# Loading the early pair's table rows, and using them, three token tiles later

## The chip, the cores and the metric

The kernel runs on one core of one Trainium2 chip. The metric is the device time of one execution in microseconds; it is given as the median of three runs. Beside these there is one execution that the hardware profiler recorded, and all views of the profile are of that one.

## The reference

The program is an attention over pooled keys and values, followed by a layer of experts in which each token that passes a test goes to one expert out of eight.

```python
def _attn_ref(q, k, v):                       # 8 batches, 8 heads, 576 tokens, 64
    k_p = k.reshape(B, H, Sp, pool, D).mean(axis=3)          # pool = 8, Sp = 72
    v_p = v.reshape(B, H, Sp, pool, D).mean(axis=3)
    scores = scale * np.matmul(q, k_p.transpose(0, 1, 3, 2))
    attn = softmax(scores)
    return np.matmul(attn, v_p)

def _moe_ref(x, w_skip, w_gate, w1, w2):      # x: 4608 tokens of 512; 8 experts, F = 1024
    do_compute = x @ w_skip > 0
    out = x.copy()
    xc = x[do_compute]
    logits = xc @ w_gate
    e_idx = np.argmax(logits, axis=1)
    gate_w = softmax(logits)[arange, e_idx]
    for e in range(E):
        mask = e_idx == e
        h = np.maximum(xc[mask] @ w1[e], 0.0)
        y[mask] = gate_w[mask, None] * (h @ w2[e])
    out[do_compute] = xc + y
    return out
```

## The kernel before

The 4608 tokens are 36 tiles of 128. `attention` goes over them in a loop, `for t in range(NT)`, as a software pipeline written out by hand: in step t PE makes the scores of tile t (L295), ACT the exponentials of tile t - 1 (L309), PE the transposes of tile t - 2 (L320, L325), PE the products with v of tile t - 4 (`values`, L339 and L341, into the one PSUM tile `o`), and DVE normalises tile t - 5 (`normalised`: L353, L355, L359, L360). L360 writes the finished tile into `x`, a pool tile with three buffers, and L361 stores it on SP's queue into the result `out`.

PE, ACT and DVE run in the order of this code. POOL and SP take their work in the order in which it was given to them, each from a queue of its own. SP carries q (L283), k (L189), v (L217, L218), the weights of the first expert (L521), those of the second (L530), and the stores of x (L361). POOL pools v (L229 to L231), adds halves of k (L205), makes the low parts of the weights (`w2lo`, L540), places part of v (`vbd`, L272), and issues the indirect DMAs.

Beside this runs the routing, in groups of tiles (`GROUPS`, 6 tiles at first). `route` takes a group's logits through a chain of small DVE steps, a few in each t, and then scatters the token numbers and gate weights of each tile into a table in DRAM that is sorted by expert (`table`, L415, one indirect DMA for a tile on POOL's queue).

After 18 tiles (`EARLY`), the third group, `near_tokens` prepares a head start: the first 256 rows of the table belong to the first expert in `ORDER`, so a pair of 128-token tiles can be taken up before the routing is finished. L428 loads these rows into `near["ids"]` (`nids` in the trace) on SP's queue, L443 makes row numbers (`near["slot"]`, `nslot`) on DVE, and L445 gathers the two tiles of tokens from `out` into `ring[:, 3]` and `ring[:, 4]` by two indirect DMAs on POOL's queue. The DVE part and the gathers are put into `later` and run `NWAIT` = 3 steps of t after the last of the small steps of `near_tokens`.

What uses `ring` comes later: in the last two steps of the loop (t = 34, 35) `tx` transposes the two tiles on PE (L472) and copies them into `xhi` and `xlo`, and after the loop `products` runs the first layer (L482 to L484) and the second (L497 to L499) of that pair, between the last tiles' small steps. Then the table is complete, `slots` plans the rest, and `experts` works through all the experts' tokens.

Of the kernel before, what the change touches and what calls it, by code (L numbers as in the profile page):

```python
# [70 lines left out]
QUARTERS = 288, 320, 352, 384  # L71
HALF = 64
BIT = 3
NWAIT = 3
WARM = 3
SLOTS = 3 * (MAXU + 2)
NO_TOKEN = 1 << 20
# [81 lines left out]
def attention(tc, nc, q, k, vm, vr, cf, w1, w2, whi, wlo, out, c, pay, offs, table, load_constants, near, bufs, late, early, fin):  # L159
    with ExitStack() as ctx:  # L160
# [207 lines left out]
        def route(t0, n):  # L368
# [51 lines left out]
            if t0 + n == EARLY:  # L420
                yield from near_tokens()

        def near_tokens():

            count = offs[:, 0:1]
            less = ap.tile([128, 1], F32, name="less")
            nn = ap.tile([128, 1], F32, name="nn")
            nc.sync.dma_start(near["ids"], table[0:256].rearrange("(s l) t -> l s t", l=128))  # L428
            nc.vector.tensor_scalar(nn, count, 256.0, 2.0, ALU.is_ge, ALU.mult)
            yield  # L430
            nc.vector.tensor_scalar(less, count, 256.0, float(NO_TOKEN), ALU.is_lt, ALU.mult)
            yield
            nc.vector.tensor_scalar(near["first"][:, 0:1], nn, 128.0, None, ALU.mult)
            yield
            nc.vector.tensor_scalar(near["jt"][:, 0:1], nn, -1.0, float(JT), ALU.mult, ALU.add)
            yield
            nc.vector.tensor_tensor(near["place"], c["place"], nn, ALU.add)

            late("ring")
            nc.gpsimd.memset(bufs["ring"], 0.0)  # L440

            def gathers():
                nc.vector.tensor_scalar(near["slot"], near["ids"][:, :, 0], less, None, ALU.add)  # L443
                for i in range(2):
                    nc.gpsimd.indirect_dma_start(bufs["ring"][:, 3 + i, 0:D], None, out[0:EARLY * 128],  # L445
                                                 bass.IndirectOffsetOnAxis(ap=near["slot"][:, i:i + 1], axis=0),
                                                 bounds_check=EARLY * 128 - 1, oob_is_err=False)
            later[t + NWAIT] = gathers
            yield

        later = {}
# [232 lines left out]
        t = NT - 1  # L684
# [538 lines left out]
```

## Time and profile before

| what | value |
|---|---|
| median of three runs | 585.3 us (581.41, 585.3, 587.0) |
| the profiled execution | 581.93 us, its span 580.1 us |
| PE busy | 519.9 us (90% of the span) |
| PE weight loads busy | 466.2 us (80%) |
| DVE busy | 313.2 us (54%) |
| ACT busy | 245.2 us (42%) |
| POOL busy | 235.2 us (41%) |
| mean granted clock of PE | 0.957 |
| moved by DMA | 86.06 MB, mean 148 GB/s |

The span is the time from the first to the last instruction of the profiled execution; what is left to its time lies around it. A row of a timeline reads: start in us, duration in us, engine, line of the kernel, operation, what is written from what, the shape, how many such instructions were merged; in brackets the idle time ahead of it and what ended that. SPq is the sequencer that issues SP's DMAs. A row of a view of windows has, for each engine, its busy time in the window and the count of its instructions.

### The profile page before, as it was taken

The page shows a single profiled execution, that of the slowest core. Times are in us where ns is not written, and L with a number is a line of the kernel's source. Part 1 is how long each engine was busy: PE and PEld are TensorE (multiplying, and loading weights), DVE is VectorE, ACT ScalarE, POOL GpSimd, SP SyncE. Part 2 cuts the span into 40 slices and gives each one's busy share as a digit, 9 for nine tenths or more (in the row PEclk, how much of TensorE's full clock was granted, in tenths as well). Part 3 has the DMA queues.
Part 4 walks back from the last instruction along what each step waited for, and adds up shares of the span by engine and source line. Part 5 has one row for each costly group of instructions (what it writes and reads, how often), then busy time and mean ns, then how long its engine had stood idle before and what let it go on. Part 6 is the DMA issues. An engine that isn't in the chain of part 4 may idle for free. (4 is left out here: it accounts for less than half of the span.)

```text
span 580.1 us, 11104 instructions
## 1 busy us (share of the span) xinstructions
PE 519.9 (90%) x3347; PEld 466.2 (80%) x3348; DVE 313.2 (54%) x750; ACT 245.2 (42%) x672; POOL 235.2 (41%) x315
## 2 busy tenths in 40 slices
PE   8499978877499977699999999999999999999993
PEld 5398867767489956688898989989989898989892
DVE  3768778878367652124453545322363648465562
ACT  5478766758396101114141424212243436343440
POOL 4869386768852733111232123323242024204132
PEclk9799989879799998899999999999999999999998
DMA  8958996952768111001541235101144537562200
GB/s 300 398 219 294 317 193 251 238 206 78 254 198 239 57 38 44 7 20 57 201 156 56 74 145 185 60 31 52 54 142 170 187 117 255 184 236 97 91 26 7
DMA packets 33450, 86.06 MB, mean 148 GB/s; under 512 B 7486, under 2 KB 7747, under 8 KB 31489
## 3 DMA queue, kind: packets, MB, share of 16 engines
q1 hardware_dynamic: 25312, 71.62, 37.2%
q0 software_dynamic: 8096, 13.95, 7.1%
q8 instruction: 20, 0.33, 0.3%
q14 instruction: 22, 0.17, 0.1%
HBM read 73.79 MB, written 20.52 MB: 163 GB/s over the span
## 5 line engine op out<-in xcount | busy, mean ns | idle before, releaser
L1019 PE MATMUL psl<-xhi,w1hi 128*128 128x256 f32 (+3 forms) x416 | 122.7, 295 | 5.0 <-PEq L874 4.9
L1020 PE MATMUL psl<-xlo,w1hi 128*128 128x256 f32 (+3 forms) x416 | 122.1, 294 | 0.0
L1021 PE MATMUL psl<-xhi,w1lo 128*128 128x256 f32 (+3 forms) x416 | 122.0, 293 | 0.0
L949 POOL DMA_INDIRECT out<-ring,slot x39 | 39.4, 1011 | 188.3 <-POOLq L874 185.5
L1076 ACT ACTIVATE hhi<-psl 128x256 fp32r<-128x256 f32 (+4 forms) x104 | 42.0, 404 | 157.0 <-ACTq L874 155.9
L1033 PE MATMUL psf<-w2hi,hhi 128*128 128x512 f32 x240 | 96.7, 403 | 6.2 <-PEq L874 6.2
L1034 PE MATMUL psf<-w2lo,hhi 128*128 128x512 f32 x240 | 95.3, 397 | 0.0
L1133 DVE SCALAR_TENSOR_TENSOR hlo<-psl,hhi 128x256 fp32r<-128x256 f32 (+2 forms) x104 | 43.7, 422 | 80.6 <-DVEq L874 80.4
L1019 PEld LDWEIGHTS psl<-xhi,w1hi 128*128 128x128 f32 x416 | 78.8, 190 | 6.5 <-issue 5.9
L1036 PE MATMUL psf<-w2hi,hlo 128*128 128x512 f32 x200 | 79.6, 398 | 0.0
L1020 PEld LDWEIGHTS psl<-xlo,w1hi 128*128 128x128 f32 x416 | 78.9, 190 | 0.6
L1021 PEld LDWEIGHTS psl<-xhi,w1lo 128*128 128x128 f32 x416 | 78.9, 190 | 0.0
L339 PE MATMUL o<-vbd,pT 128*128 128x148 f32 (+1 forms) x304 | 54.1, 318 | 20.8 <-DVE x L360 17.5
L309 ACT ACTIVATE e<-sc,nm 128x72 f32<-128x72 f32 x288 | 64.8, 343 | 16.3 <-DVE nm L302 16.0
L1122 DVE SCALAR_TENSOR_TENSOR ring<-psf,ring 128x512 f32 x25 | 18.7, 749 | 83.9 <-DVEq L874 83.9
L339 PEld LDWEIGHTS o<-vbd,pT 128*128 128x128 f32 (+1 forms) x304 | 44.7, 197 | 23.5 <-issue 16.7
L1033 PEld LDWEIGHTS psf<-w2hi,hhi 128*128 128x128 f32 x240 | 45.5, 190 | 16.5 <-issue 6.6
L1034 PEld LDWEIGHTS psf<-w2lo,hhi 128*128 128x128 f32 x240 | 45.5, 190 | 9.9
L1085 ACT ACTIVATE xhi<-psd 128x512 fp32r<-128x512 f32 x36 | 18.9, 598 | 75.5 <-ACTq L874 75.5
L944 POOL DMA_INDIRECT ring<-out,slot x39 | 44.4, 1139 | 15.2 <-issue 12.9
L415 POOL DMA_INDIRECT table<-pay,r_di x36 | 35.7, 991 | 33.7 <-DVE rc L355 11.5
L1036 PEld LDWEIGHTS psf<-w2hi,hlo 128*128 128x128 f32 x200 | 37.9, 189 | 9.2
(207 smaller groups left out, 909.9 us busy)
## 6 DMA issues: line engine op xcount, KB each, us to landing
stage<-in_w SPq DMA_DIRECT2D x64, 512.0 KB, 4.4
out<-x SPq DMA_DIRECT2D x36, 256.0 KB, 4.9
stage<-in_k SPq DMA_DIRECT2D x7, 1152.0 KB, 9.8
hlo<-in_vm SPq DMA_DIRECT2D x4, 1024.0 KB, 8.4
hhi<-in_vm SPq DMA_DIRECT2D x4, 1024.0 KB, 5.4
xlo<-in_q SPq DMA_DIRECT2D x6, 512.0 KB, 6.7
qt<-in_q SPq DMA_DIRECT2D x6, 512.0 KB, 6.0
xhi<-in_q SPq DMA_DIRECT2D x5, 512.0 KB, 6.9
```

The costliest lines, as they stand in the source:

```text
L309: nc.scalar.activation(e[:, h, :], sc[h // 4][:, h % 4 * SP:(h % 4 + 1) * SP], AF.Exp, bias=nm[:, h:h + 1], scale=-1.0)
L339: nc.tensor.matmul(o_[sl, g * 2 * VA:(g + 1) * 2 * VA], pT[:, 2 * a + g, sl], vbd[b % 3][:, 2 * a + g, :], start=(g == 0), stop=False)
L944: g.indirect_dma_start(ring[:, s % 6, 0:D], None, out, bass.IndirectOffsetOnAxis(ap=slot[:, s:s + 1], axis=0), bounds_check=NTOK - 1, oob_ ...
L949: g.indirect_dma_start(out, bass.IndirectOffsetOnAxis(ap=offsets, axis=0), ring[:, s % 6, 0:D], None, bounds_check=NTOK - 1, oob_is_err=Fa ...
L1019: t.matmul(ps, whi[0][:, k, w], xhi[:, k, xs], start=(k == 0), stop=False)
L1020: t.matmul(ps, whi[0][:, k, w], xlo[:, k, xs], start=False, stop=False)
L1021: last = t.matmul(ps, wlo[0][:, k, w], xhi[:, k, xs], start=False, stop=(k == 3))
L1033: t.matmul(ps, hhi[:, k, sl], whi[1][:, k, :], start=(k == 0), stop=False)
L1034: last = t.matmul(ps, hhi[:, k, sl], wlo[1][:, k, :], start=False, stop=(short and k == 7))
L1036: last = t.matmul(ps, hlo[:, k, sl], whi[1][:, k, :], start=False, stop=(k == 7))
L1076: a.activation(hhi[:, f, xs], psL[f % 3][:, xs], AF.Relu).then_inc(sem["act"], 1)
L1133: m = v.scalar_tensor_tensor(to[:, f], psL[f % 3][:, cs], 0.0, hhi[:, f, cs].bitcast(F32), ALU.max, ALU.subtract)
```

## The change

The load of the table rows is taken out of the first of `near_tokens`' small steps and put into `later`, two steps of t (`NIDS`) after the last of them; the slot numbers and the gathers go from three steps after it to six.

```diff
-NWAIT = 3
+NIDS = 2
+NWAIT = 6
...
             nn = ap.tile([128, 1], F32, name="nn")
-            nc.sync.dma_start(near["ids"], table[0:256].rearrange("(s l) t -> l s t", l=128))
             nc.vector.tensor_scalar(nn, count, 256.0, 2.0, ALU.is_ge, ALU.mult)
...
             nc.gpsimd.memset(bufs["ring"], 0.0)
+
+            def ids():
+                nc.sync.dma_start(near["ids"], table[0:256].rearrange("(s l) t -> l s t", l=128))
 
             def gathers():
                 nc.vector.tensor_scalar(near["slot"], near["ids"][:, :, 0], less, None, ALU.add)
...
+            later[t + NIDS] = ids
             later[t + NWAIT] = gathers
             yield
```

The order of PE and of ACT stays as it was. On SP's queue, from the v load of the last batch (`hhi`, `vl`) on, the order before is this; `nids` is the load that moves, `stage<-in_w` are weights, `xhi`, `xlo` and `qt` with `in_q` are loads of q, and `out<-x` are stores of finished tiles:

```order
L217 DMA hhi<-in_vm 128x2048
L218 DMA vl<-in_vr 64x512
L428 DMA nids<-table 128x2x2
L521 DMA stage<-in_w 128x2x512
L283 DMA xhi<-in_q 128x1024
L361 DMA out<-x 128x512 x2
L521 DMA stage<-in_w 128x2x512
L283 DMA xlo<-in_q 128x1024
L361 DMA out<-x 128x512 x2
L283 DMA qt<-in_q 128x1024
```

And with the change (lines after the edit are four higher, one higher ahead of it):

```order
L218 DMA hhi<-in_vm 128x2048
L219 DMA vl<-in_vr 64x512
L525 DMA stage<-in_w 128x2x512
L284 DMA xhi<-in_q 128x1024
L362 DMA out<-x 128x512 x2
L525 DMA stage<-in_w 128x2x512
L284 DMA xlo<-in_q 128x1024
L362 DMA out<-x 128x512
L443 DMA nids<-table 128x2x2
L362 DMA out<-x 128x512
L284 DMA qt<-in_q 128x1024
```

The load of the table rows has gone behind two weight loads, two loads of q and three stores of x (tiles 21, 22 and 23).

On POOL's queue, at the end of the loop's work, the order before is this; `ring<-out,nslot` are the two gathers, `table<-pay,r_di` the scatters of the fourth routing group:

```order
L540 TENSOR_TENSOR w2lo<-stage,w2hi 128x512
L445 DMA ring<-out,nslot 128x512 x2
L272 TENSOR_TENSOR vbd_121<-gs,cfs 128x8x9
L275 TENSOR_TENSOR vl_124<-gs,cfs 64x4x9
L540 TENSOR_TENSOR w2lo<-stage,w2hi 128x512
L415 DMA table<-pay,r_di 36864x2 x6
L540 TENSOR_TENSOR w2lo<-stage,w2hi 128x512 x2
L272 TENSOR_TENSOR vbd_122<-gs,cfs 128x8x9
```

And with the change:

```order
L544 TENSOR_TENSOR w2lo<-stage,w2hi 128x512
L273 TENSOR_TENSOR vbd_121<-gs,cfs 128x8x9
L276 TENSOR_TENSOR vl_124<-gs,cfs 64x4x9
L544 TENSOR_TENSOR w2lo<-stage,w2hi 128x512
L416 DMA table<-pay,r_di 36864x2 x6
L544 TENSOR_TENSOR w2lo<-stage,w2hi 128x512 x2
L448 DMA ring<-out,nslot 128x512 x2
L273 TENSOR_TENSOR vbd_122<-gs,cfs 128x8x9
```

The gathers have gone behind the six scatters and three pieces of w2lo, and stand right ahead of the last batch's vbd. On DVE the one instruction that makes `nslot` has gone three steps of t later with them.

## The prediction

> **What bounds the kernel now.** I read the page's slices first, then SyncE's own waits, then the timelines of SP, DVE and PE around the one place that stands out, then POOL's timeline and the landings of its DMAs at the place to which work moves.
>
> ```profile
> span 580.1 us, 11104 instructions
> PE   8499978877499977699999999999999999999993
> SPq L428 <- DMA table<-pay,r_di: 15.1, 1, 15.1
> 129.49 0.47 SPq L218 DMA_DIRECT2D vl<-in_vr  x1
> 145.15 0.39 SPq L428 DMA_DIRECT2D nids<-table  x1
> 147.69 0.86 SPq L361 DMA_DIRECT2D out<-x  x2
> ```
>
> One slice is 14.5 us. From the eighteenth on PE is at nine tenths or more: the expert part is bound by PE and isn't touched by the change. The attention part before it has low slices, of which the eleventh, 145 to 160 us, is at four tenths. SP's queue explains that one: it meets the load of the table rows (nids, L428) at 130.0 us, and stands there for 15.1 us until the scatters into the table have landed. Behind it stand a weight load (L521), a load of q, and the stores of the finished token tiles (L361), which come out at 147.69.
>
> ```profile
> 141.80 0.68 DVE L360 TENSOR_TENSOR x<-o,rc 128x512 f32<-128x512 f32 x1
> 146.79 0.22 DVE L359 TENSOR_TENSOR l<-o,rc 128x72 f32<-128x72 f32 x1
> 153.28 0.69 DVE L360 TENSOR_TENSOR x<-o,rc 128x512 f32<-128x512 f32 x1 [6.27 <-DMA out<-x]
> 142.65 0.72 PE L339 MATMUL o<-vbd,pT 128*128 128x148 f32 x4
> 144.21 0.65 PE L295 MATMUL sc<-kbd,qt 128*128 128x144 f32 x4
> 144.70 0.60 PE L320 MATMUL pt<-cfs,e 128*128 128x128 f32 x4
> 145.84 0.76 PE L295 MATMUL sc<-kbd,qt 128*128 128x144 f32 x4
> 154.12 1.33 PE L339 MATMUL o<-vbd,pT 128*128 128x148 f32 x4 [7.53 <-DVE x L360]
> 157.22 1.03 PE L295 MATMUL sc<-kbd,xhi 128*128 128x144 f32 x4
> 158.08 0.30 PE L397 MATMUL mps<-r_oh,ones 128*128 128x56 bf16 x6
> ```
>
> This is the price. The tile x has three buffers; DVE's L360 may write tile 24 only when the store of tile 21 has landed, and that store left at 147.69 instead of soon after its x was ready. DVE waits 6.27 us, PE 7.53.
>
> **What the change takes away.** In the new order SP passes straight from the vl load to the weight load, the q load and the stores of tiles 21 and 22, then a weight load, a q load and the store of tile 23 before it meets nids. Tile 21's store can leave some 18 us before tile 24 needs the buffer (x of tile 24 is due at about 147). So L360 starts right behind L359, 0.15 us after its start as in the other tiles: 146.79 + 0.15 = 146.94 instead of 153.28, that is 6.34 us. There is a second part: after the gap PE runs slowly.
>
> ```profile
> 152.00:156.00 4.00, 1.88 (x8) 1.91 (x9) 2.49 (x9) 1.63 (x8) 2.62 (x3) 0.50 1.04 410
> 156.00:160.00 4.00, 4.00 (x31) 3.79 (x30) 1.64 (x7) 1.24 (x5) 2.10 (x2) 0.75 0.62 237
> ```
>
> The seventh figure after the window is the granted clock (0.50, then 0.75); the last two are DMA share and GB/s. The block of L339 and L341 takes 157.22 - 154.12 = 3.10 us there against 144.21 - 142.65 = 1.56 at full clock, and the scores behind it 158.08 - 157.22 = 0.86 against 144.70 - 144.21 = 0.49. That is 1.54 + 0.37 = 1.9 us that go too. **Term 1: -6.3 - 1.9 = -8.2 us.** What else is moved earlier here (two weight loads, two q loads) goes into a DMA that is quiet, and POOL's pooling of v that ran beside the stall now runs beside DVE, which I take to cost nothing that shows.
>
> ```profile
> 141.22 0.98 POOL L415 DMA_INDIRECT table<-pay,r_di  x1 [0.30 <-issue]
> 142.20 2.54 POOL L540 TENSOR_TENSOR w2lo<-stage,w2hi 128x512 fp32r<-128x512 f32 x2
> ```
>
> Nids itself now meets SP at about 145: the weight load ahead of it waits for a buffer that the first of these two w2lo sets free, at 143.5. The last scatter that nids needs is issued at 141.22 and had landed by 145.1, so with that landing SP hardly stops. Behind it stand the stores of tiles 24 and 25, a q load, and the first loads of the next expert's weights, none due for several us. I take 0; a rival below prices it.
>
> **What the change puts in its place.** The two gathers into ring (L445) leave POOL's place after w2lo and come behind six scatters of the next routing group and two more w2lo; DVE's one small L443 goes along and I take nothing for it. What uses the gathers doesn't move: the transposes of ring (L472) in the last two token tiles. On the old times, POOL and PE stand so there:
>
> ```profile
> 156.09 1.09 POOL L445 DMA_INDIRECT ring<-out,nslot  x1 [1.46 <-DVE nslot L443]
> 166.31 1.04 POOL L415 DMA_INDIRECT table<-pay,r_di  x1 [3.02 <-DVE pay L413]
> 172.80 0.98 POOL L415 DMA_INDIRECT table<-pay,r_di  x1 [0.30 <-issue]
> 173.79 2.52 POOL L540 TENSOR_TENSOR w2lo<-stage,w2hi 128x512 fp32r<-128x512 f32 x2
> 176.25 0.32 POOL L272 TENSOR_TENSOR vbd<-gs,cfs 128x72 f32<-128x72 f32 x1
> 175.83 0.60 PE L472 MATMUL mps<-cfs,ring 128*128 128x128 f32 x4
> 180.72 0.77 PE L339 MATMUL o<-vbd,pT 128*64 128x148 f32 x6 [0.44 <-DVE x L360]
> ```
>
> Both sides move 8.2 us earlier alike (POOL's scatters start at DVE's pay), so I compare them on the old times. The first gather is issued at about 176.3, when w2lo ends: PE wants its rows at 175.83. It is late before it has begun. When it lands is the question of this prediction. Alone, the two gathers took as the first line here says; a scatter takes as the second:
>
> ```profile
> DMA to landing us min/median/max: 2.1/2.6/3.1
> DMA to landing us min/median/max: 2.1/6.6/13.5
> table<-pay,r_di POOLq DMA_INDIRECT x1, 9.2
> table<-pay,r_di POOLq DMA_INDIRECT x1, 5.5
> table<-pay,r_di POOLq DMA_INDIRECT x1, 4.4
> table<-pay,r_di POOLq DMA_INDIRECT x1, 3.3
> 196.02 0.98 POOL L415 DMA_INDIRECT table<-pay,r_di  x1 [0.30 <-DVE r_cm L387]
> 198.59 0.98 POOL L415 DMA_INDIRECT table<-pay,r_di  x1 [0.30 <-issue]
> ```
>
> The third line is the scatter issued at 172.80, the sixth of the group that the gathers now follow: it lands at 182.0, with the weight loads of the next expert in flight. The next three are the scatters issued at 196.02, 197.31 and 198.59: they land at 201.5, 201.7 and 201.9, one closely behind the other. So DMAs of POOL's queue land in their order, and one behind a backlog comes out 0.2 us or so after the one ahead. I choose this over the lone gather's 2.6 us, because the new place is behind just such a group: the gather lands at 182.0 + 0.3 = 182.3. **Term 2: PE waits 182.3 - 175.8 = +6.5 us** at L472, with ACT, in order, behind it at the copy of those transposes. Bounds: +2.6 (a landing 2.1 us after issue) and +10.8 (the 13.5 us of the second line, 172.8 + 13.5 + 0.3 = 186.6). The second gather is wanted 3.8 us after the first and lands by then. On POOL the vbd of the last batch (L272) now stands behind two gathers, 1.09 + 0.3 + 1.0 = 2.4 us: 178.7 instead of 176.25, ahead of the L339 at 180.72 that needs it.
>
> **Term 3: the clock after that wait.** The gap of 7.53 us cost 1.9 us of slow PE. Shorter gaps went both ways:
>
> ```profile
> 110.65 1.32 PE L339 MATMUL o<-vbd,pT 128*128 128x148 f32 x4 [2.40 <-DVE x L360]
> 135.82 0.75 PE L339 MATMUL o<-vbd,pT 128*64 128x148 f32 x6 [2.93 <-DVE x L360]
> 136.00:140.00 4.00, 4.00 (x42) 3.79 (x41) 2.59 (x11) 2.76 (x11) 3.01 (x4) 1.00 0.06 3
> ```
>
> After 2.40 us the four L339 took 1.32 us, as slow as after the long gap; after 2.93 us the clock stayed at 1.00. Bounds 0 and 1.9; 6.5 us is nearest to 7.53, so **+1.9 us**.
>
> The Trainium skill, "TensorE: Matmul & The Clock Gate", Part 1, says that the PE clock falls to half after an idle window of about 3.4 us. This trace shows a fall after 2.40 us, so the row is stricter than the rule. By the rule a wait of 3.2 us, as in the first rival, would cost no clock.
>
> **Sum:** -8.2 + 6.5 + 1.9 = +0.2 us. The profiled execution took 581.93 us (span 580.1), so the sum is 582.1 on its own time. The three runs shown (581.41, 585.3, 587.0) and the profiled one have a mean of 583.9; with the sum that is **584.1 us**. No change, in other words: one long stall of PE traded for another.
>
> **Rivals.**
> The gather isn't held by the scatters. It lands 2.6 us after its issue, at 178.9, PE waits 3.1, and the clock costs half of its bounds, 1.0: -8.2 + 3.1 + 1.0 = -4.1, 579.8 us. For it: the lone gathers at 156 landed so right behind a stretch in which the DMA share was 1.04. Against it: the order of landings above.
>
> The Trainium skill, "DMA: Bandwidth & Descriptors", "Anatomy of one DMA — SWDGE (gpsimd) path", gives such a DMA about 2.0 us fixed and the bytes at 436 GB/s. An estimate from it for 256 KB is 2.6 us, which speaks for this rival; the scatters of this trace, with few bytes, took a median of 6.6.
>
> The same, and the drain gains. While PE waits, the last weight loads clear, and the scatters of the next groups find an empty DMA.
>
> ```profile
> 201.38 0.16 DVE L411 TENSOR_TENSOR r_di<-r_ds,r_no 128x2 int32<-128x2 f32 x1 [2.79 <-DMA table<-pay,r_di]
> ```
>
> This wait of 2.79 us for a landing then goes: -4.1 - 2.8 = -6.9, 577.0 us. Against it: six stores of x are in flight there before and after.
>
> Slower: a longer backlog. If the sixth scatter lands as the slowest of the first group did, PE waits 10.8: -8.2 + 10.8 + 1.9 = +4.5, 588.4 us. It decides from a wait of 6.3 us on, so from a landing at 182.1 on the old times, and the forecast sits just there. For it: one weight load now comes after the following store, so into the scatters' time. Against: 9.2 is what this group did.
>
> Slower: the stall stays at nids. The scatters that nids waits for landed 3.9 us after the last issue (141.22 to 145.1) in a DMA that SP's own stop kept empty; now loads run beside them. If the last one takes 13.5 us, SP is held until 154.7, the store of tile 24 lands 5.6 us later (as 147.69 to 153.28), at 160.3, and x of tile 27 (167.25 before, so 159.1) waits 1.2 us. With a clock loss of 1.9 the sum is 0.2 + 1.2 + 1.9 = +3.3, 587.2 us.
>
> ```profile
> 167.25 0.68 DVE L360 TENSOR_TENSOR x<-o,rc 128x512 f32<-128x512 f32 x1
> ```
>
> **How the numbers follow.** Forecast 0.38; gather not held 0.20; with the drain's gain 0.10; longer backlog 0.26; nids still blocking 0.06. One per cent, about what a measurement of this kernel can tell from no change, is 5.8 us. The case with the drain's gain is past it; of the first rival and the two slower ones, 4 to 5 us from nothing, I count a third to a half beyond it, since the runs of one kernel lie 5.6 us apart. That gives faster 0.2, same 0.6, slower 0.2. The range runs from the case with the drain's gain to the longer backlog, widened by the 3 us by which the runs lie about their mean: 576.5 to 591.5.
>
> **What would show it.** Right: SP's 15.1 us at nids shrinks to a few us, and tile 24's L360 has no wait for a store; PE's 7.53 us at L339 are gone; the transposes of ring wait 5 to 8 us for the gather, which lands 5 us or more after its issue; the granted clock is at half just behind. Wrong: a gather landing 2 to 3 us after issue behind the six scatters (term 2 too large), a gap at L339 for x in the tiles 24 to 27 (term 1 too large), or full clock after the new gap.

## The result and the profile after

The changed kernel took 588.2 us (median of 22 runs, 584.92 to 591.79) where the kernel before took 586.0 us beside it (22 runs, 581.41 to 589.02). The ratio is 1.0064 with a 95% interval of 1.0041 to 1.0087: slower by 3.7 us (2.4 to 5.1). Each ratio here is taken over the runs within 1.5% of their kernel's fastest, and it need not equal that of the medians (here 1.0038). The time lies inside the predicted range, but it isn't "no change".

The page's span and PE's slices of the changed kernel:

```profile
span 589.9 us, 11103 instructions
PE   7589978878866985879999999999999999999993
```

The four at 145 to 160 us is gone: the eleventh slice (147 to 162) is at eight tenths. The twelfth and the thirteenth, 162 to 192, have fallen from nine tenths to six. SyncE's own waits and its timeline tell why the four went:

```profile
SPq L525 <- POOL w2lo L544: 3.9, 1, 3.9
149.82 1.10 SPq L362 DMA_DIRECT2D out<-x  x1
151.03 0.38 SPq L443 DMA_DIRECT2D nids<-table  x1
151.50 0.83 SPq L362 DMA_DIRECT2D out<-x  x1
```

There is no wait at nids (L443) any more: it goes out 0.1 us after the store ahead of it. The 15.1 us at L428 have become 3.9 us at a weight load whose buffer w2lo frees. On PE's timeline:

```profile
139.41 0.74 PE L340 MATMUL o<-vbd,pT 128*64 128x148 f32 x6 [2.93 <-DVE x L361]
151.34 0.74 PE L340 MATMUL o<-vbd,pT 128*128 128x148 f32 x4 [1.15 <-DVE x L361]
154.24 0.30 PE L398 MATMUL mps<-r_oh,ones 128*128 128x56 bf16 x6 [0.67 <-DVE rs L354]
182.01 1.09 PE L476 MATMUL mps<-cfs,ring 128*128 128x128 f32 x4 [9.77 <-DMA ring<-out,nslot]
182.89 1.19 PE L340 MATMUL o<-vbd,pT 128*128 128x148 f32 x4
185.69 0.65 PE L296 MATMUL sc<-kbd,qt 128*128 128x144 f32 x4
210.04 0.47 PE L501 MATMUL sc<-w2hi,hhi 128*128 128x512 f32 x1 [0.52 <-DVE s_three L787]
```

The 7.53 us ahead of tile 24's products are 1.15 us, and a wait of 9.77 us for the gather stands ahead of the transposes of ring. The two executions that the profiler recorded differ already ahead of the change, so I measure from a row that is the same in both, the one whose idle time is 2.93 us: 135.82 before, 139.41 after. From there PE is ready for ring's transposes at 175.83 - 135.82 = 40.0 us before, and at 182.01 - 9.77 - 139.41 = 32.8 after: 7.2 us earlier. In the kernel before, the scores behind those transposes (which answer to the row at 185.69) and the second layer of the early pair start at

```profile
177.78 0.65 PE L295 MATMUL sc<-kbd,qt 128*128 128x144 f32 x4
202.93 0.47 PE L497 MATMUL sc<-w2hi,hhi 128*128 128x512 f32 x1 [0.81 <-DVE s_three L783]
```

The second layer starts 67.1 us after the measuring row before, and 70.6 us after it in the changed kernel: 3.5 us later, in line with the 3.7 us of the ratio. I use this distance, from the row with L339 or L340 to the first product of the second layer, for the experiments too.

POOL's timeline and the landings of its transfers (the last figure of such a row is the time from issue to landing):

```profile
169.04 0.98 POOL L416 DMA_INDIRECT table<-pay,r_di  x1 [0.30 <-issue]
170.03 2.51 POOL L544 TENSOR_TENSOR w2lo<-stage,w2hi 128x512 fp32r<-128x512 f32 x2
172.71 1.06 POOL L448 DMA_INDIRECT ring<-out,nslot  x1 [0.16 <-issue]
table<-pay,r_di POOLq DMA_INDIRECT x1, 10.3
ring<-out,nslot POOLq DMA_INDIRECT x1, 9.2
```

The sixth scatter, issued at 169.04, lands at 179.3; the first gather, issued at 172.71, lands at 181.9, 2.6 us behind it. The view of windows shows what the DMA did meanwhile (the last three figures are the granted clock, the mean busy share of the DMA engines, and GB/s; the share can come out above 1, as in the second row):

```profile
168.00:170.00 2.00, 2.00 (x18) 2.00 (x17) 0.81 (x3) 1.98 (x10) 1.70 (x2) 1.00 0.94 64
172.00:174.00 2.00, 0.24 (x2) 0.02 (x1) 0.46 (x1) 1.12 (x4) 1.60 (x2) 1.00 1.13 387
182.00:184.00 2.00, 1.99 (x9) 2.00 (x10) 0.24 (x1) 0.87 (x3) 0.00 (x0) 0.50 0.06 25
160.00:182.00 22.00, 12.20 (x100) 11.28 (x98) 8.90 (x32) 11.96 (x46) 11.00 (x12) 0.85 0.85 213
```

At 168 to 170 the engines move 64 GB/s at a busy share of 0.94, at 172 to 174 they move 387. The gather lands as this traffic ends, at about 182, and PE then starts at half clock.

### The profile page after: what moved, and what is told of

Its sections match the earlier page's. It is cut to its first block, busy times and chain, and to the rows that moved or that the text cites. A ratio compares the mean times of both kernels' runs of the same rounds, so it can differ in the third digit from the quotient of the medians.

```text
span 589.9 us, 11103 instructions
## 1 busy us (share of the span) xinstructions
PE 523.0 (89%) x3347; PEld 468.8 (79%) x3348; DVE 316.6 (54%) x750; ACT 245.1 (42%) x672; POOL 234.4 (40%) x315
## 5 line engine op out<-in xcount | busy, mean ns | idle before, releaser
L340 PE MATMUL o<-vbd,pT 128*128 128x148 f32 (+1 forms) x304 | 54.0, 317 | 14.9 <-DVE x L361 10.6
L340 PEld LDWEIGHTS o<-vbd,pT 128*128 128x128 f32 (+1 forms) x304 | 44.7, 197 | 17.5 <-issue 9.3
## 6 DMA issues: line engine op xcount, KB each, us to landing
stage<-in_k SPq DMA_DIRECT2D x7, 1152.0 KB, 10.7
```

The source lines that it names most:

```text
L340: nc.tensor.matmul(o_[sl, g * 2 * VA:(g + 1) * 2 * VA], pT[:, 2 * a + g, sl], vbd[b % 3][:, 2 * a + g, :], start=(g == 0), stop=False)
```

## The experiments

The theory: the removed stall is worth what was forecast, and the gathers behind the scatters cost more than it, because scatters that write and the next expert's weight loads are in flight together there. The rivals: the row load's later place does the harm; the loads alone do it; the scatters alone do it; the gather's own bytes do it.

### Each half of the change alone

The first kernel leaves the row load where the change puts it, and takes the gathers back in front of the fourth group's scatters.

```diff
 NIDS = 2
-NWAIT = 6
+NWAIT = 4
```

> The change with the gathers four steps after near_tokens instead of six, so ahead of the scatters of the fourth routing group on POOL's queue. Theory (two opposite terms: the stall at the load of the table rows goes, 7 to 8 us; the wait of PE for the gather, 9.8 us in the changed kernel's profile, is the price of standing behind the scatters): the gain alone is left, ratio to before 0.985 to 0.990, no gap above 2 us at L340 for x, and no wait at the transposes of ring. Rival 1 (later table rows cost something else, such as SP stopping at nids in a fuller DMA): ratio 0.997 or more. Rival 2 (the gather takes 9 us wherever it stands once the loads run): a wait of PE of 3 us or more at the transposes, ratio about 0.995.

Measured: 577.9 us (6 runs) against 584.2, ratio 0.985 (0.975 to 0.994). PE doesn't wait at ring's transposes, and the slowdown turns into a gain, as the theory had it. The second does the other half: the kernel before, its row load where it was, with only the gathers late.

```diff
-NWAIT = 3
+NWAIT = 6
```

> The other half: the table rows are loaded where the kernel before loads them, the gathers come six steps after. Theory (the terms add): SP's 15 us at nids and PE's gap of 7.5 us stay, and PE waits 9 to 11 us more at the transposes of ring: ratio to before 1.016 to 1.020. Rival (the two stalls share a cause, so that SP's stop takes traffic away from the scatters and shortens the second): ratio 1.010 or less, with a wait at the transposes under 6 us.

Measured: 592.6 us (6 runs), ratio 1.014 (1.005 to 1.022), between what the two sides had expected. The trace decides: SP stands at nids for 15.9 us, and on PE's timeline both stalls are there, the second just under the 9 to 11 us expected:

```profile
154.54 1.32 PE L339 MATMUL o<-vbd,pT 128*128 128x148 f32 x4 [7.80 <-DVE x L360]
185.41 1.08 PE L472 MATMUL mps<-cfs,ring 128*128 128x128 f32 x4 [8.89 <-DMA ring<-out,nslot]
```

So the halves are independent: moving the row load removes the one wait, moving the gathers makes the other, and neither cures nor causes the other's.

### No weight loads in flight

The changed kernel with the eight weight loads of the second expert (L534) put behind the store of tile 30 on SP's queue; nothing else is touched.

```diff
-            nc.sync.dma_start(out[t * 128:(t + 1) * 128, :], flat(x))
+            stores[t] = nc.sync.dma_start(out[t * 128:(t + 1) * 128, :], flat(x)).ins
...
-                nc.sync.dma_start(chunk_view(stage[:, cc], cc), chunk_src(w1, w2, 1, cc))
+                m = nc.sync.dma_start(chunk_view(stage[:, cc], cc), chunk_src(w1, w2, 1, cc))
+                tc.add_manual_dep(m.ins, stores[30].name, ...)
```

> The changed kernel, but the eight loads of the second expert's weights stand on SP's queue behind the store of token tile 30, so that none is in flight while the six scatters and the gathers are. Theory (the scatters land late because those loads run beside them, and the gather comes behind them): the sixth scatter lands 3.5 to 5 us after its issue as the third group's did in the kernel before (3.9), the gather about 2.5 us after its own, PE waits 2.5 to 3.5 us instead of 9.8; about 6 us less than the changed kernel, if the loads don't slow the fifth group's scatters: ratio to before 0.992 to 1.000. Rival (scatters are slow by themselves, loads or not): the wait stays 8 us or more, ratio 1.005 or more.

Measured: 582.2 us (12 runs) against 584.2; the ratio is 1.005 (1.000 to 1.010), where the theory had 0.992 to 1.000. The medians point the other way, so the time is left open. The wait in the trace isn't. POOL's gather, its landing, PE, and the windows:

```profile
172.02 1.06 POOL L448 DMA_INDIRECT ring<-out,nslot  x1 [0.16 <-issue]
ring<-out,nslot POOLq DMA_INDIRECT x1, 2.2
174.32 0.63 PE L476 MATMUL mps<-cfs,ring 128*128 128x128 f32 x4 [2.76 <-DMA ring<-out,nslot]
174.79 0.67 PE L340 MATMUL o<-vbd,pT 128*128 128x148 f32 x4
168.00:170.00 2.00, 2.00 (x18) 2.00 (x18) 1.07 (x6) 1.31 (x7) 1.68 (x3) 1.00 0.20 54
198.91 0.21 PE L398 MATMUL mps<-r_oh,ones 128*128 128x24 bf16 x2 [2.96 <-DVE r_oh L392]
```

In the same place behind the same six scatters, the gather now takes 2.2 us from issue to landing in place of 9.2, and PE waits 2.76 us and keeps its full clock (0.67 us for four products, not 1.19). The scatters are still slow: the fourth and the fifth of them take 6.6 and 5.8 us, where 3.5 to 5 was expected of the sixth, whose landing isn't in this trace; in the changed kernel they take 11.9 and 10.8. The fifth lands at 172.9 and the gather at 174.2, so the gather is at most 1.3 us behind the sixth.

The gain doesn't reach the second layer in this execution. It starts at 204.86, 70.5 us after the row with the idle time of 2.93 us (here at 134.41), as late as in the changed kernel. Two things took most of it: PE was ready for ring 37.1 us after that row and not 32.8, since its clock was low at 134 to 138 and at 148 to 152 (0.65 and 0.60), ahead of all that the edit moves; and there is the new wait of 2.96 us. DVE stood there for 4.08 us ahead of L361 (at 196.28) until a store of x had landed, and on SP's queue the stores now stand among the moved loads.

### Scatters that write nothing

The changed kernel, but the fourth group's row numbers are all out of bounds, so that its six scatters are issued and write nothing; the experts' part of these 768 tokens is left out.

```diff
-            nc.vector.tensor_tensor(di, ds, no, ALU.add)
+            if t0 + n == 24:
+                nc.vector.tensor_scalar(di, ds, 1.0, float(NO_TOKEN), ALU.mult, ALU.add)
+            else:
+                nc.vector.tensor_tensor(di, ds, no, ALU.add)
```

> The changed kernel, but the six scatters of the fourth routing group get row numbers past the table's end, so that they are issued at the same times on POOL and write nothing (the experts' part of those 768 tokens is left out of the result; the counts, and so the experts' loop, stay). Theory (the gather lands late because it stands behind scatters that write): the scatters land 2 to 4 us after issue, the gather 2.5 to 3.5 us after its own with the loads of weights still in flight, PE waits 3 to 4 us: about 6 us less than the changed kernel, ratio 0.994 to 0.998. Rival (the loads in flight alone make the gather slow, whatever it stands behind): the gather lands 8 us or more after its issue, and the ratio stays at 1.005 or more.

Measured: 582.3 us (12 runs), ratio 0.999 (0.995 to 1.003). The median is that of the kernel without loads in flight, while the two ratios, to the same runs of the kernel before, differ by 0.006: times don't tell these two kernels apart. The landings of the sixth scatter and of the gather, PE, and the windows that answer to the first and the last of the four above (the gather is issued 2.2 us earlier here, so they are moved by as much):

```profile
table<-pay,r_di POOLq DMA_INDIRECT x1, 4.8
ring<-out,nslot POOLq DMA_INDIRECT x1, 4.6
175.20 1.09 PE L479 MATMUL mps<-cfs,ring 128*128 128x128 f32 x4 [5.13 <-DMA ring<-out,nslot]
165.80:167.80 2.00, 2.00 (x18) 2.00 (x17) 0.77 (x3) 2.00 (x10) 1.70 (x2) 1.00 0.94 304
157.80:179.80 22.00, 16.87 (x121) 15.99 (x119) 10.85 (x42) 13.96 (x53) 10.99 (x12) 0.86 0.67 215
```

With the same loads and no rows written, the engines move 304 GB/s at the same busy share of 0.94, in place of 64. Over the 22 us they move as much as before (215 and 213 GB/s) in 0.67 of the time in place of 0.85, so by this estimate the writes had cost them 0.18 x 22 = 4.0 us. The sixth scatter lands 4.8 us after its issue in place of 10.3, and the gather 4.6 in place of 9.2. PE's wait lies between what the two sides had expected, so each was half right: neither the writes nor the loads alone make the 9.8 us, which fall to 5.1 without the one and to 2.8 without the other. These waits can be compared, since PE is ready 0.4 to 0.5 us ahead of the gather's issue in all three: 172.24 and 172.71, 171.56 and 172.02, 170.07 and 170.49. The second layer again starts no earlier (72.6 us after the measuring row, here at 132.10): PE was ready for ring after 38.0 us, with its clock at 0.51 behind that row, which has a gap of 5.22 us here, and at 0.62 at 152 to 156.

### The gather's own bytes, and its distance

The changed kernel with gathers of 32 numbers for each row number in place of 512. They are taken from the first 144 tokens, of which each holds 16 such pieces, so the places read lie closer together as well.

```diff
-    nc.gpsimd.indirect_dma_start(bufs["ring"][:, 3 + i, 0:D], None, out[0:EARLY * 128],
+    nc.gpsimd.indirect_dma_start(bufs["ring"][:, 3 + i, 0:32], None, out[0:EARLY * 8].rearrange("a (b d) -> (a b) d", d=32),
```

> The changed kernel, but the two gathers fetch 32 columns of each row in place of 512 (16 KB each in place of 256 KB, the same 128 rows), so that the first expert's early pair works on other numbers. In the changed kernel the first gather landed 2.6 us behind the sixth scatter. If that is the gather's own bytes, moved beside the weight loads, it now lands at most 0.6 us behind the sixth, PE waits 7.3 to 7.9 us in place of 9.8, and the ratio to the kernel before is 1.001 to 1.005. Rival: the cost is one of rows or of the queue and not of bytes; then it lands 2 to 3 us behind as before, PE waits 9 to 10, and the ratio stays 1.004 to 1.009.

Measured: 588.3 us (6 runs) against 583.3, ratio 1.012 (1.008 to 1.016). POOL, the two landings, and PE:

```profile
166.86 0.97 POOL L416 DMA_INDIRECT table<-pay,r_di  x1 [0.30 <-issue]
170.53 1.05 POOL L448 DMA_INDIRECT ring<-out,nslot  x1 [0.17 <-issue]
table<-pay,r_di POOLq DMA_INDIRECT x1, 9.0
ring<-out,nslot POOLq DMA_INDIRECT x1, 7.8
132.98 0.74 PE L340 MATMUL o<-vbd,pT 128*64 128x148 f32 x6 [2.88 <-DVE x L361]
134.01 0.70 PE L340 MATMUL o<-vbd,pT 128*64 128x148 f32 x4
147.46 1.04 PE L340 MATMUL o<-vbd,pT 128*128 128x148 f32 x4 [2.09 <-DVE x L361]
178.43 1.09 PE L476 MATMUL mps<-cfs,ring 128*128 128x128 f32 x4 [8.32 <-DMA ring<-out,nslot]
```

The sixth scatter lands at 175.9 and the gather at 178.3, 2.4 us behind it, with a sixteenth of the bytes: the bytes aren't what holds it, and the expectation put first was wrong. The wait of 8.3 us lies between the two sides. That the kernel is slower than the changed one isn't shown, since the two intervals overlap (1.008 to 1.016 and 1.004 to 1.009). But in this execution too PE came late to ring: from 132.98 it is ready after 178.43 - 8.32 - 132.98 = 37.1 us, not 32.8, so 4.3 us went ahead of the gathers, where the code is the same. PE's clock took most of it. From 134.01 on, a microsecond after PE had resumed, products are slow: four take 0.70 us. In the changed kernel the same four, behind its row at 139.41, take 0.47:

```profile
140.44 0.47 PE L340 MATMUL o<-vbd,pT 128*64 128x148 f32 x4
```

Up to the next fast products (138.28 here, 143.09 there) that cost 5.3 - 3.7 = 1.6 us. The clock fell again by 147.46, after a gap of 2.09 us, where four products take 1.04 us and 0.74 (at 151.34) in the changed kernel. The kernel without loads in flight lost its 4.3 us at the same two places.

The Trainium skill, "DMA: Bandwidth & Descriptors", "Queues, rings and completion order", says that a DMA engine takes the queues that have work in turn, packet by packet, and that a transfer's semaphore is raised only after every earlier write of that engine, on whatever queue. By that rule a gather of few bytes would still land only when the loads' earlier writes had; the narrow gather agrees (7.8 us), and so does the gather without loads (2.2 us). No run here shows which of the two statements, if either, does it.

The other kernel shortens the distance: the gathers come one token tile earlier, still behind the scatters but between the two w2lo.

```diff
-NWAIT = 6
+NWAIT = 5
```

> The changed kernel with the gathers one token tile earlier: still behind the six scatters, but ahead of the second of the two w2lo, so issued 1.3 us earlier. If the queue's order sets the landing, the first gather still comes out 2 to 3 us behind the sixth scatter, some 12 us or more after that one's issue, PE still waits 9 to 10 us, and the ratio is 1.004 to 1.009. Rival: a gather takes its own 9 us from its issue; then it lands 1.3 us earlier, at most 1.5 us behind the sixth, PE waits about 8.5, and the ratio is 1.001 to 1.006.

Measured: 585.2 us (12 runs), ratio 1.002 (0.998 to 1.007). The landing of the fifth scatter (issued at 161.33), POOL, the gather's landing, and PE:

```profile
table<-pay,r_di POOLq DMA_INDIRECT x1, 10.0
162.61 0.98 POOL L416 DMA_INDIRECT table<-pay,r_di  x1 [0.30 <-issue]
165.07 1.06 POOL L448 DMA_INDIRECT ring<-out,nslot  x1 [0.17 <-issue]
ring<-out,nslot POOLq DMA_INDIRECT x1, 7.3
132.83 1.28 PE L340 MATMUL o<-vbd,pT 128*64 128x148 f32 x6 [5.52 <-DVE x L361]
172.47 1.09 PE L476 MATMUL mps<-cfs,ring 128*128 128x128 f32 x4 [6.61 <-DMA ring<-out,nslot]
```

The gather is issued 2.5 us after the sixth scatter in place of 3.7, and lands 9.8 us after that issue in place of 12.9: PE waits 6.6 us, less than either side had said. The landing of the sixth scatter itself isn't in this trace, but the fifth lands at 171.3, so the gather, at 172.4, is at most 1.1 us behind the sixth: within the rival's 1.5, and not the 2 to 3 us that the queue's order was taken to give. Issued earlier it does land earlier, so the queue's order alone doesn't set the landing. But its flight isn't a fixed 9 us either (7.3 here), and this is one execution.

### The gathers in front, once more

The first experiment's kernel, measured once more.

> The kernel with the gathers ahead of the fourth group's scatters once more, since its first ratio had a wide interval (0.975 to 0.994). Theory: only the removed stall is left of the change, -8.2 us by the prediction's first term and -7.2 as measured, so the ratio is 0.985 to 0.989; the gathers land 2 to 5 us after their issue and the transposes of ring wait for nothing. Rival: the pair's gathers now delay the scatters of the fourth group, whose landing holds up the fifth group's chain, and half of the gain goes: 0.992 to 0.995.

Measured: 575.8 us (9 runs) against 583.3, ratio 0.9865 (0.9817 to 0.9912). On POOL the second gather stands directly ahead of the first scatter; its landing, and PE:

```profile
151.24 1.03 POOL L448 DMA_INDIRECT ring<-out,nslot  x1 [0.16 <-issue]
ring<-out,nslot POOLq DMA_INDIRECT x1, 3.9
129.10 0.74 PE L340 MATMUL o<-vbd,pT 128*64 128x148 f32 x6 [2.95 <-DVE x L361]
161.67 0.60 PE L476 MATMUL mps<-cfs,ring 128*128 128x128 f32 x4
188.78 0.47 PE L501 MATMUL sc<-w2hi,hhi 128*128 128x512 f32 x1 [0.82 <-DVE s_three L787]
```

PE is at ring's transposes 32.6 us after the row at 129.10, as in the changed kernel (32.8), and doesn't wait. The second layer starts after 59.7 us, 7.4 less than before. The ratio gives 7.9 us (5.1 to 10.7). By the ratios this version is faster than both kernels.

## Why the prediction was wrong

**Term 1, right in its cause, 1.0 us too large.** Forecast -8.2, measured -7.2 at ring's transposes, and -7.4 in the trace with the gathers in front, where PE doesn't wait at ring. SP no longer stops at nids, tile 24 waits for no store, and the slow products behind the gap are fast (0.74 us, not 1.33). The wait is as forecast: from the measuring row to tile 24's products it is 154.12 - 135.82 = 18.3 us before and 151.34 - 139.41 = 11.9 after, 6.4 less. Of the 1.9 us of slow PE only 0.8 came; a part of the rest is the wait of 0.67 us for DVE at 154.24, which the kernel before doesn't have. These are single executions: where the clock falls on the way, as in the two experiments above with 37.1 us to ring, the gain up to there is 2.9 us. One reading was wrong without effect: tile 21's store could leave some 11 us ahead of need, not 18, as its x is written at 135.00.

**Term 2, the mechanism right and the size wrong: this is the step that failed.** Forecast was a wait of 6.5 us, measured 9.77. That PE would be ready about when the gather is issued was right: it was issued 172.71 - 172.24 = 0.5 us after, as forecast (176.3 against 175.83). The landing was built of two figures, and both were too small. The sixth scatter was given the 9.2 us that it had taken before; it took 10.3. And the gather was put 0.3 us behind it, as three scatters of the fifth group come out that are issued 1.3 us apart; it came 2.6 behind. Together that is 1.1 + 2.3 = 3.4 us, against 9.77 - 6.5 = 3.3 missing. The step from "the scatters land one closely behind the other" to "the gather does too" was the weak one: the gather is another transfer, issued 3.7 us after the sixth scatter, with POOL's two w2lo between. Its bytes aren't the cause (2.4 us behind with a sixteenth of them). What fixes the distance stays open. It isn't a constant: 2.8 us in the kernel with only the gathers late, 3.5 behind scatters that write nothing, at most 1.1 with the gathers one token tile earlier, and at most 1.3 without the loads, where the gather's whole flight is 2.2. What the runs do show is that the landing comes of two things together, scatters that write and loads in flight: the wait is 9.8 us with both, 5.1 without the writes and 2.8 without the loads.

**Term 3, right.** Forecast +1.9. From ring's transposes to the scores that are fast again PE takes 185.69 - 182.01 = 3.7 us, and before 177.78 - 175.83 = 1.95: the half clock cost 1.7 us. Behind that some 0.8 us came back, which no term has: the wait of 0.44 us that the kernel before has at 180.72 is gone, and that ahead of the second layer is 0.52 in place of 0.81.

**Sum.** -7.2 + 9.8 + 1.7 - 0.8 = +3.5 us where +0.2 was forecast; the ratio says +3.7. Of the rivals, the longer backlog (+4.5, with a wait of 10.8 us) is nearest, by the landing that the prediction named as its point: 182.1 on the old times, measured 181.9 - 139.41 + 135.82 + 7.2 = 185.5. Its cause came only in part: the sixth scatter took 1.1 us longer, not 4.3, and the larger share is the gather's distance behind it. The gather not held by the scatters didn't come in the changed kernel, but it is what the trace without loads shows (2.2 us after issue, a wait of 2.76, full clock). The drain's gain and the stall that stays at nids weren't seen.

Before the runs the two sides of the sum were known only to 8 us in term 2, and the middle of its bounds (6.7) would have been no better than the figure chosen. But a nearer row than the fifth group's was in the trace: the last three scatters of the fourth group itself landed at 180.7, 181.0 and 182.0, so up to 1.0 us apart and not 0.2. Two figures of the prediction don't follow from its own: 577.0 widened by 3 us is 574.0 and not 576.5, and the first rival's wait is 3.1 us and not 3.2. Neither bears on the result.

## What to carry to other kernels

A transfer moved out of a queue's way is free only if its new place is quiet: look at which transfers fly at that time, on all queues, before taking a landing from a quiet stretch or from the transfer ahead. If a move has two halves, one that removes a wait and one that only follows, cost each by itself: here the row load had to go later, while the gathers that use it could go one token tile later and stop in front of the next scatters. To compare two profiled executions, measure from a row just ahead of the change; here that row stood 3.6 us later in the changed kernel, as much as the effect. And look at the granted clock on the way, which made most of a difference of 4.3 us between executions.

## What the hardware showed that I had not expected

Six scatters of 128 rows of 8 bytes cost the DMA engines some 4.0 us of busy time beside the loads, by the estimate above; at worst the engines moved 64 GB/s at a busy share of 0.94, where the same share without the writes moved 304.

The flight of one gather of 256 KB went from 2.2 us (no loads) over 4.6 (loads, nothing written) to 9.2 (both). The Trainium skill, "DMA: Bandwidth & Descriptors", "Anatomy of one DMA — SWDGE (gpsimd) path", gives about 2.0 us and the bytes at 436 GB/s, an estimate of 2.6 us. The first is near it, and for the last it isn't a price.

The length of a gap doesn't settle PE's clock. The same products stand behind a gap of the same length in the first experiment's kernel (first line) and in the changed one:

```profile
113.08 0.74 PE L340 MATMUL o<-vbd,pT 128*128 128x148 f32 x4 [2.39 <-DVE x L361]
114.03 1.32 PE L340 MATMUL o<-vbd,pT 128*128 128x148 f32 x4 [2.38 <-DVE x L361]
```

The granted clock is 1.00 behind the first (at 113 to 115) and 0.50 behind the second (at 114 to 116). After 2.93 us it stayed in the changed kernel (0.74 at 139.41, then 0.47), and after 2.88 us in the narrow gathers' kernel it fell a microsecond after PE had resumed. I take this for a part of why runs of one kernel lie several us apart; that wasn't tested.
